# Fifty instead of thirty softmax tiles transposed by DMA, buffers named step by step, and a new order of steps

## The chip, the core and the metric

The kernel runs on one core of one Trainium2 chip. TensorE (PE) does the matrix products, VectorE (DVE), ScalarE (ACT) and GpSimd (POOL) the elementwise work, and SyncE (SP) issues nearly all DMAs. Every engine runs its own instructions in the order in which they are written, and waits on semaphores for the others. The metric is the time of one execution in device microseconds; lower is better.

## The reference, cut to what matters

Clustered attention (a query sees only the keys whose nearest centroid is the same as its own), then two feed-forward blocks on its output. Both weights and activations are float32, and the result has to keep nearly that precision.

```python
q_assign = np.argmax(np.einsum('bhsd,hcd->bhsc', q_n, c_n), axis=-1)   # B, H, S, D, C = 2, 8, 768, 64, 16
k_assign = np.argmax(np.einsum('bhsd,hcd->bhsc', k_n, c_n), axis=-1)
mask = q_assign[:, :, :, None] == k_assign[:, :, None, :]
scores = scale * np.matmul(q, k.transpose(0, 1, 3, 2))
scores = np.where(mask, scores, -1000000000.0)
scores = scores - np.max(scores, axis=-1, keepdims=True)
attn = np.exp(scores)
attn = attn / (np.sum(attn, axis=-1, keepdims=True) + 1e-09)
x = np.matmul(attn, v)             # then to [1536 tokens, 512]
h = x @ w_in                       # 512 x 2048
x = np.where(h > 0, h, np.exp(np.minimum(h, 0)) - 1) @ w_out
out = ((x @ w_a) * (x @ w_b)) @ w_out2   # 512 x 1536 twice, 1536 x 512
```

## The kernel before

**One list of steps.** The whole program is one list of words, `ORDER`, such as `tr:4.3.1`. A loop at the end of the kernel takes word after word and calls the function of that name with these numbers, which emits one step, on one engine or on SP's DMA queue. Nothing else orders the work: each engine runs its own steps in the order of the list, and a step waits only for the data and the buffers that it needs. A last number often says which engine takes the step: 0 is DVE, 1 ACT, 2 POOL.

**Attention.** There are 16 heads (batch times head), handled as 8 pairs, and each head has 6 tiles of 128 queries against all 768 keys, 96 tiles in all. For a tile `t` of head `g`:

- `sc` (PE, L673): the scores, four matmuls into one of two buffers in PSUM; the second two of them bring the cluster mask in.
- `rm` (DVE, L681): the negated row maximum.
- `ex` (ACT, L694): the exponential, float32, into `pf`, which has three buffers for all heads.
- Then the tile is split into two float16 parts, a high one and the remainder, and both are brought to keys-by-queries in `pt`, where the product with V reads them. This goes **one of two ways**.
  By PE: `tr` (PE, L727) transposes half of the tile, three 128x128 blocks, into PSUM; `th` (L731) copies that to float16 as the high part, and `tl` (DVE, L736) takes the remainder. A tile has two halves, so two `tr`, two `th`, two `tl`.
  By DMA: `hi` (L702, ACT or POOL) rounds the whole tile to float16 in `phl`, `lo` (POOL, L709) writes the remainder beside it, and `td` (SP, L741) is one DMA that transposes both parts into `pt`. Here `pf` stays taken until `lo` has read it.
- `av` (PE, L786): the product with V, for three tiles of both heads of a pair at a time (a "half", `f` 0 or 1), in three steps; `rb` (PE, L767) and `ev` (DVE) bring the division by the row sums in.

Besides these, each head needs its operands: `ka1`, `ka2` (the key and its rounding remainder, L523 and L530), `qa` (L545), `qb` (L484), `kbd` (a DMA), `vs`, `v1`, `v2` (V scaled and in two float16 parts, L491, L496, L501); `sm`, `st`, `m1` to `m5`, `oh`, `ohs`, `ohd` find the clusters.

**Weights.** Each weight comes in 68 pieces as int64 words (`wl`, a DMA). `wa` (ACT), `w0` to `w4` (DVE), `wh` (ACT), `ws` and `wq` (POOL, L905 and L911) turn a piece into a high and a low part. The first pieces are made during attention.

**The two MLPs.** `h`, `x2`, `ab` and `o` are the matrix products in three passes (high by high, low by high, high by low; L925 to L927).

Buffers come from `take`. A tag with several buffers hands them out in turn. The head of the program also has 60 steps `wm`, eight small matmuls each, that fill PE while it waits for the first data.

Of the kernel before, what the change touches and what calls it, by code (L numbers as in the profile page):

```python
# [65 lines left out]
lk:1.1 lk:0.0 wm:0 wm:2 lq:1.1 cz:0 lq:0.0 ib:0 wm:4 wm:6 cs:0 wm:7 wm:10 vl:2 wm:11 wl:0 mo:0 wm:15  # L66
kb:1 md:0 vl:3 wm:14 wm:19 ka1:0.1 vl:1 sb:0 wm:22 vl:0 ka1:1.1 kb:0 wm:25 wm:27 ka2:0.2 qa:1.1
ka2:1.0 wm:28 wm:29 wm:26 lk:2.0 c0:0 wm:33 qa:0.1 lk:3.0 wm:37 c1:0 ce:0 wm:38 qb:0 wm:5 wm:20 qb:1
wm:46 wm:48 c2:0 lq:2.0 vr:9 wm:24 wm:53 vr:10 wm:55 lq:3.0 vr:8 wm:17 vr:11 c3:0 wm:42 wa:0 c4:0
wm:49 wm:57 wm:23 wm:30 w0:0 sm:0.0 w1:0 vr:14 w2:0 vr:13 w3:0 sm:0.1 vr:12 w4:0 vr:15 sv:0.0.0 wh:0  # L70
wm:31 sv:0.1.0 wm:56 ws:0 vr:5 st:0 vr:6 vr:4 wq:0 wm:40 m1:0 vr:7 wm:13 m2:0 wm:45 vr:0 wm:16 m3:0
wm:1 vr:3 wl:1 m4:0 ka1:3.2 wm:39 vr:1 ka1:2.2 vr:2 vtp:0 m5:0 wm:18 wm:58 ka2:2.2 vtd:0 ot:0 oe:0
ot:2 wm:8 oe:2 wm:3 wm:47 wm:41 vbp:0 wm:52 sc:0.0 vbd:0 ot:3 rm:0.0 sc:0.1 qa:3.1 qa:2.1 wm:51
ka2:3.2 vs:1 wm:21 qb:2 ot:1 rm:0.1 oe:1 ex:0.0 oe:3 tr:0.0.1 sc:0.2 ex:0.1 rm:0.2 wa:1 qb:3 w0:1
wm:54 wm:50 lq:4.0 tr:0.1.0 th:0.0.1.1 sc:1.0 ex:0.2 th:0.1.0.1 hi:0.2.2 tl:0.0.1 wm:59 tr:0.0.0
sc:1.1 tl:0.1.0 rm:1.0 rm:1.1 tr:0.1.1 th:0.0.0.1 sm:1.0 th:0.1.1.1 vs:2 tl:0.1.1 ex:1.0 sc:1.2 vs:0
ex:1.1 tl:0.0.0 tr:1.0.1 sv:1.0.1 rm:1.2 th:1.0.1.1 vs:3 lo:0.2 w1:1 v1:0.1 sc:0.3 v2:0.2 kbd:3
rm:0.3 ex:1.2 wm:44 tl:1.0.1 w2:1 lq:5.0 tr:1.0.0 wm:12 th:1.0.0.1 v1:1.1 tr:1.1.0 th:1.1.0.1 sc:0.4
wm:9 tl:1.0.0 wm:36 rm:0.4 ra:0.0 ex:0.3 w3:1 w4:1 rc:0.0 tr:1.1.1 lk:4.0 th:1.1.1.1 sm:1.1 sc:0.5
hi:1.2.1 tl:1.1.1 ex:0.4 sv:1.1.1 wm:34 st:1 tl:1.1.0 rm:0.5 qa:4.1 wm:32 kbd:2 lo:1.2 ka1:4.2  # L80
v1:2.1 wh:1 ex:0.5 td:0.2 tr:0.3.0 sc:1.4 wm:35 rx:0.0 tr:0.3.1 sc:1.3 lk:5.0 th:0.3.0.1 m1:1
hi:0.5.1 m2:1 th:0.3.1.1 v2:1.2 v2:2.2 m3:1 m4:1 ka2:4.2 m5:1 tl:0.3.0 wm:43 oh:1 rm:1.3 ohs:1
tr:0.4.0 ex:1.3 tl:0.3.1 rm:1.4 ws:1 qb:4 th:0.4.0.1 td:1.2 av:0.0.0 rb:0.0 ohd:1 tr:0.4.1 sc:1.5
re:0.0.1 th:0.4.1.1 wl:2 tl:0.4.0 rm:1.5 tl:0.4.1 ex:1.4 qa:5.1 wq:1 tr:1.3.0 th:1.3.0.1 tr:1.3.1
av:0.0.1 th:1.3.1.0 tr:1.4.1 lq:7.0 ex:1.5 th:1.4.1.1 lo:0.5 ra:0.1 tl:1.3.1 sc:2.0 tl:1.3.0 rm:2.0
hi:1.5.1 tr:1.4.0 sc:2.1 ex:2.0 av:0.0.2 ka1:5.2 vs:4 lo:1.5 td:0.5 tl:1.4.1 rm:2.1 sc:2.2 tr:2.0.0
th:1.4.0.1 rc:0.1 tr:2.0.1 tl:1.4.0 ex:2.1 th:2.0.0.1 th:2.0.1.1 rx:0.1 lk:6.0 sc:3.0 rm:2.2 ex:2.2
# [1053 lines left out]
```

## Time and profile before

| | |
|---|---|
| Time, median of 3 runs | 818.26 us (817.41 to 818.92) |
| The profiled execution | 818.15 us |
| Its span, first to last instruction | 816.4 us |
| PE busy | 807.5 us, 99% of the span |
| DVE, ACT, POOL busy over the span | 592.6, 410.8, 340.7 us |
| Softmax tiles that go by DMA | 30 of 96 |

The span is the time between the first and the last instruction on the core; 1.75 us of the execution lie around it. The transposes of attention run from 33.9 us to 259.1 us, the products with V from 54.3 us, and the first product of the MLP begins at 252.6 us. Shares over the whole span mix two stages: after attention PE alone is full, while in attention the other engines are nearly full as well. So each stretch has to be read by itself.

### The profile page before, as it was taken

Reading aid. Unit: us, or ns where it says so; the run is one execution under the profiler, and the core shown is the slowest. Engines: PE = TensorE matmul, PEld = TensorE weight load, DVE = VectorE, ACT = ScalarE, POOL = GpSimd, SP = SyncE. Lnnn points to the kernel's source line nnn. Section 1 sums busy time; section 2 is a strip of 40 time slices with the busy share of each in tenths; the row PEclk is TensorE's granted clock in tenths of the full one; section 3 lists DMA queues with packets and bytes.
Section 4 is the critical chain, followed back from the end, with each engine's and each line's share of the span. In section 5 each row is a group of like instructions: output and inputs, shape, how many; then the busy total and the mean of one; then the engine's idle time right before and its main releaser. Section 6 shows DMA issues by size and latency. Waiting matters only on the chain.

```text
span 816.4 us, 12164 instructions
## 1 busy us (share of the span) xinstructions
PE 807.5 (99%) x4626; PEld 655.4 (80%) x4626; DVE 592.6 (73%) x876; ACT 410.8 (50%) x737; POOL 340.7 (42%) x295
## 2 busy tenths in 40 slices
...
GB/s 278 110 97 129 146 125 110 129 138 116 110 81 78 78 27 78 77 104 78 79 95 81 80 60 72 52 77 78 1 26 77 78 78 52 53 52 0 52 1 103
DMA packets 65626, 68.12 MB, mean 83 GB/s; under 512 B 49888, under 2 KB 49888, under 8 KB 65568
## 3 DMA queue, kind: packets, MB, share of 16 engines
q1 hardware_dynamic: 65328, 66.76, 30.6%
...
q10 hardware_dynamic: 240, 0.59, 0.3%
...
## 4 chain that ended last, share of the span: by engine, by line
PE 90%; POOL 5%; ACT 3%; issue 2%; DVE 0%; POOLq 0%; ACTq 0%
PE ab L927 8%; PE ab L925 8%; PE ab L926 8%; PE sc L673 6%; PE h L926 5%; PE h L925 5%; PE x L926 5%; PE x L925 5%; PE h L927 5%; PE x L927 5%; PE av L786 4%; PE o L927 4%; PE o L925 4%; PE o L926 4%; PE tt L727 4%; PE warm_ps L409 3%
## 5 line engine op out<-in xcount | busy, mean ns | idle before, releaser
L681 DVE TENSOR_REDUCE nm<-sc 128x1 f32<-128x768 f32 x96 | 90.8, 950 | 7.1 <-PE sc L673 6.0
L694 ACT ACTIVATE pf<-sc,nm 128x768 f32<-128x768 f32 x96 | 86.8, 905 | 15.7 <-POOL phl L709 6.9
L1027 ACT COPY t0ab<-ab 128x512 f32<-128x512 f32 x36 | 21.1, 587 | 108.5 <-PE ab L927 108.5
L736 DVE TENSOR_TENSOR pt<-tt,pt 128x384 f16<-128x384 f32 x132 | 70.0, 545 | 5.0 <-ACT pt L731 4.6
L1032 DVE TENSOR_TENSOR t1ab<-ab,t0ab 128x512 f32<-128x512 f32 x36 | 24.8, 688 | 63.2 <-ACT t0ab L1027 63.2
L727 PE MATMUL tt<-identf,pf 128*128 128x128 f32 x396 | 62.0, 277 | 1.4 <-ACT pf L694 1.4
L731 ACT CAST pt<-tt 128x384 f16<-128x384 f32 x122 | 55.9, 478 | 10.4 <-PE tt L727 9.8
L709 POOL TENSOR_TENSOR phl<-pf,phl 128x768 f16<-128x768 f32 x30 | 50.0, 1668 | 24.8 <-ACT phl L702 23.5
L673 PE MATMUL sc<-ka,qa 128*128 128x384 f32 x192 | 57.6, 381 | 2.5 <-ACT pf L694 2.4
L856 ACT ACTIVATE wg<-wraw 128x512 f32<-128x512 f32 x68 | 45.1, 667 | 25.5 <-DMA wraw<-in_w_out_dram 13.8
L727 PEld LDWEIGHTS tt<-identf,pf 128*128 128x128 f32 x396 | 46.0, 140 | 12.0 <-issue 4.3
L786 PE MATMUL av<-pt,v 128*64 128x384 f16 x576 | 52.7, 329 | 0.0
L873 DVE SCALAR_TENSOR_TENSOR wf<-wraw,wg 128x512 int32<-128x512 int32 x68 | 51.0, 751 | 1.8
L886 DVE SCALAR_TENSOR_TENSOR wg<-wraw,wg 128x512 f32<-128x512 uint32 x68 | 49.1, 723 | 1.7
L673 PE MATMUL sc<-kb,qb 80*128 80x384 f32 x192 | 49.6, 339 | 0.0
L1043 DVE TENSOR_TENSOR gl<-t1ab,gh 128x512 fp32r<-128x512 f32 x36 | 33.9, 941 | 18.7 <-ACT gh L1038 18.5
L861 DVE TENSOR_SCALAR wg<-wg 128x512 f32<-128x512 f32 x68 | 38.4, 566 | 8.8 <-ACT wg L856 8.6
L786 PEld LDWEIGHTS <-v 128*64 128x64 f16 x576 | 30.0, 109 | 18.4 <-issue 7.1
L866 DVE TENSOR_SCALAR wg<-wg 128x512 int32<-128x512 int32 x68 | 38.5, 567 | 1.8
L989 ACT CAST gh<-t1h 128x1024 fp32r<-128x1024 f32 x24 | 25.3, 1052 | 27.7 <-DVE t1h L981 27.7
L1083 DVE TENSOR_TENSOR acc<-o,acc 128x1024 f32<-128x1024 f32 (+1 forms) x12 | 14.2, 1180 | 32.3 <-PE o L927 32.3
L971 ACT ACTIVATE t0h<-h 128x1024 f32<-128x1024 f32 x24 | 24.6, 1024 | 23.3 <-PE h L927 23.2
...
## 6 DMA issues: line engine op xcount, KB each, us to landing
...
acc<-in_v_dram SPq DMA_DIRECT2D x4, 768.0 KB, 11.0
...
```

The costliest lines, as they stand in the source:

```text
L673: nc.tensor.matmul(s[:, j, :HALF], a[:, qs], b[:, j * HALF : (j + 1) * HALF], start=i == 0, stop=i == 1,)
L681: nc.vector.reduce_max(out=nm, in_=st[g][f"sc{t}"][:, :, :HALF], axis=AX.XY, negate=True)
L694: nc.scalar.activation(pf.rearrange("p (a b) -> p a b", a=2), st[g].pop(f"sc{t}")[:, :, :HALF], AF.Exp, bias=st[g].pop(f"nm{t}"), accum_ou ...
L709: nc.gpsimd.tensor_sub(phl[:, S:], st[g].pop(f"pf{t}"), phl[:, :S])
L727: nc.tensor.transpose(tt[:, k * P : (k + 1) * P], pf[:, o : o + P], identf)
L731: (nc.vector.tensor_copy, nc.scalar.copy)[e](next(parts_of(g, t, u)), st[g][f"tt{t}{u}"])
L736: nc.vector.tensor_sub(lo, st[g].pop(f"tt{t}{u}"), hi)
L786: nc.tensor.matmul(pairs[j]["av"][x * 64 : (x + 1) * 64].rearrange("p (a q) -> p a q", a=3), st[2 * j + x][("v1", "v2")[vi]][:, kt_, :], s ...
L873: nc.vector.scalar_tensor_tensor(out=f, in0=raws[n][:, :, 1], scalar=-0x40000000, in1=g, op0=ALU.bitwise_and, op1=ALU.bitwise_or,)
L925: nc.tensor.matmul(ps, lhi, rhi, start=first, stop=False)
L926: nc.tensor.matmul(ps, lhi, rlo, start=False, stop=False)
L927: nc.tensor.matmul(ps, llo, rhi, start=False, stop=last)
```

## The change

Twenty more tiles go by DMA: 50 of 96. The number of `td`, `hi` and `lo` rises from 30 to 50, and the number of `tr`, `th` and `tl` falls from 132 to 92, since each such tile has two halves. With them:

- `phl` has four buffers instead of three (`NPHL`).
- `qb` and `lo` get a last number for their engine. In the new list every `qb` stays on DVE and every `lo` on POOL.
- Some steps change engines: `hi` on ACT 12 to 34, on POOL 18 to 16. `th` on DVE 10 to 19. `ka1` on ACT 6 to 12, on POOL 10 to 4. `ka2` on DVE 1 to 6, on POOL 15 to 10. `v1` one from POOL to ACT, `sv` two and `re` three from DVE to ACT.
- A word may name buffers, as `sc:6.0/sc=0`. `take` then uses that buffer, and where a word names none, the next in turn.
- The list is in a new order. It has the same 60 `wm`, and the same number of every other step.

```diff
-NPHL = 3
+NPHL = 4
...
-qb:8 tr:4.4.0 th:4.4.1.1 sc:5.5 rm:5.4 tl:4.4.1 th:4.4.0.1 ka1:9.1 av:2.0.1 rm:5.5 tl:4.4.0 av:2.0.2
-rb:2.0 th:4.3.1.0 lo:4.5 lk:10.0 tr:5.3.0 ex:5.4 qa:9.1 ka2:9.2 ex:5.5 sc:6.0 kbd:7 tl:4.3.1
...
+ex:5.5/pf=2 ka2:9.0 rb:2.0/tt=1 hi:4.5.1/phl=2 qb:9.0 sc:6.0/sc=0 lq:11.0/rawq=1 w3:3 hi:5.5.1/phl=0
...
+    named, taken = {}, {}
+
     def take(pool, tag, shape, dt, name, bufs=1):
-        return pool.tile(shape, dt, tag=tag, bufs=bufs, name=name)
+        if bufs > 1:
+            n = taken[tag] = int(named.pop(tag, (taken.get(tag, -1) + 1) % bufs))
+            tag = f"{tag}_{n}"
+        return pool.tile(shape, dt, tag=tag, bufs=1, name=name)
...
-    def minus_scaled(out, a, scale, b):
-        nc.vector.scalar_tensor_tensor(
+    def minus_scaled(e, out, a, scale, b):
+        (nc.vector, None, nc.gpsimd)[e].scalar_tensor_tensor(
...
-    def lo(g, t):
+    def lo(g, t, e):
         phl = st[g][f"phl{t}"]
-        nc.gpsimd.tensor_sub(phl[:, S:], st[g].pop(f"pf{t}"), phl[:, :S])
+        (nc.vector, None, nc.gpsimd)[e].tensor_sub(phl[:, S:], st[g].pop(f"pf{t}"), phl[:, :S])
...
-    for word in ORDER.split():
+    for line in ORDER.split():
+        word, *buffers = line.split("/")
+        named.update(n.split("=") for n in buffers)
         name, args = word.split(":")
```

What the new list does is seen best on single engines. The place shown is the same on all three: the second half of the third pair (heads 4 and 5), at whose end head 6 begins. In a name such as `pf4_5_1991` the 4 is the tile, the 5 the head, and the last number only tells buffers apart. Line numbers after the change are 39 higher in this part of the program.

PE before, from the `rb` of that pair's first half on:

```order
L767 MATMUL rbp_2_0_1979<-identf_89,rx_2_0_1901 128x128 x3
L727 MATMUL tt30_5_1987<-identf_89,pf3_5_1925 128x128 x3
L673 MATMUL sc0_6_1998<-ka_6_1431,qa_6_1409 128x384 x2
L673 MATMUL sc0_6_1998<-kb_6_1855,qb_6_1573 128x384 x2
L727 MATMUL tt40_5_2007<-identf_89,pf4_5_1991 128x128 x3
L673 MATMUL sc1_6_2013<-ka_6_1431,qa_6_1409 128x384 x2
L673 MATMUL sc1_6_2013<-kb_6_1855,qb_6_1573 128x384 x2
L727 MATMUL tt31_5_2029<-identf_89,pf3_5_1925 128x128 x3
```

and after:

```order
L806 MATMUL rbp_2_0_1939<-identf_89,rx_2_0_1887 128x128 x3
L712 MATMUL sc0_6_1947<-ka_6_1443,qa_6_1445 128x384 x2
L712 MATMUL sc0_6_1947<-kb_6_1723,qb_6_1507 128x384 x2
L712 MATMUL sc1_6_1967<-ka_6_1443,qa_6_1445 128x384 x2
L712 MATMUL sc1_6_1967<-kb_6_1723,qb_6_1507 128x384 x2
L612 MATMUL sm_4_0_1981<-qa_8_1794,cq1_106 64x384
```

Transposes of tiles 3 and 4 of head 5 stood around the first scores of head 6. Tile 4 has left PE, tile 3 stands further ahead, and the first two scores of head 6 follow each other at once.

POOL before, between the two `rx` of the same pair (L709 is `lo`, L702 `hi`, L530 `ka2`):

```order
L757 COPY rx_2_0_1901<-rs_2_0_1770 128x384
L530 TENSOR_TENSOR ka_8_1868<-rawk_8_1797,ka_8_1868 64x768
L491 TENSOR_TENSOR acc_66<-acc_66,vsc_112 128x384
L709 TENSOR_TENSOR phl5_4_1932<-pf5_4_1870,phl5_4_1932 128x768
L530 TENSOR_TENSOR ka_9_1950<-rawk_9_1841,ka_9_1950 64x768
L702 CAST phl5_5_2021<-pf5_5_1996 128x768
L496 CAST v1_7_2026<-acc_66 128x384
L491 TENSOR_TENSOR acc_66<-acc_66,vsc_112 128x384
L709 TENSOR_TENSOR phl5_5_2021<-pf5_5_1996,phl5_5_2021 128x768
L491 TENSOR_TENSOR acc_66<-acc_66,vsc_112 128x384
L757 COPY rx_2_1_2102<-rs_2_1_2046 128x384
```

and after, between the same two `rx` (L748 is `lo`; here L530 is `vs`):

```order
L796 COPY rx_2_0_1887<-rs_2_0_1755 128x384
L748 TENSOR_TENSOR phl5_4_1943<-pf5_4_1810,phl5_4_1943 128x768
L530 TENSOR_TENSOR acc_66<-acc_66,vsc_112 128x384
L748 TENSOR_TENSOR phl5_5_1956<-pf5_5_1936,phl5_5_1956 128x768
L748 TENSOR_TENSOR phl4_5_1991<-pf4_5_1920,phl4_5_1991 128x768
L796 COPY rx_2_1_2038<-rs_2_1_1974 128x384
```

Three `lo` instead of two, two of them back to back, and the two `ka2` are gone from between: that of head 8 stands earlier on POOL, that of head 9 is on DVE.

DVE before, around the `qb` of head 9 (L736 is `tl`, L681 `rm`):

```order
L681 TENSOR_REDUCE nm4_5_1946<-sc4_5_1887 128x1
L736 TENSOR_TENSOR pt1_4_1908<-tt41_4_1897,pt1_4_1908 128x384
L681 TENSOR_REDUCE nm5_5_1964<-sc5_5_1941 128x1
L736 TENSOR_TENSOR pt1_4_1908<-tt40_4_1936,pt1_4_1908 128x384
L731 CAST pt1_4_1908<-tt31_4_1893 128x384
L736 TENSOR_TENSOR pt1_4_1908<-tt31_4_1893,pt1_4_1908 128x384
L484 SCALAR_TENSOR_TENSOR qb_9_2018<-rawq_9_1616,qa_9_1993 64x768
L736 TENSOR_TENSOR pt1_5_2005<-tt30_5_1987,pt1_5_2005 128x384
L681 TENSOR_REDUCE nm0_6_2024<-sc0_6_1998 128x1
L736 TENSOR_TENSOR pt1_5_2005<-tt40_5_2007,pt1_5_2005 128x384
L681 TENSOR_REDUCE nm1_6_2044<-sc1_6_2013 128x1
```

and after (L775 is `tl`, L720 `rm`, L569 `ka2`):

```order
L720 TENSOR_REDUCE nm4_5_1859<-sc4_5_1850 128x1
L775 TENSOR_TENSOR pt1_4_1833<-tt31_4_1789,pt1_4_1833 128x384
L720 TENSOR_REDUCE nm5_5_1885<-sc5_5_1862 128x1
L523 SCALAR_TENSOR_TENSOR qb_8_1918<-rawq_8_1566,qa_8_1794 64x768
L569 TENSOR_TENSOR ka_9_1880<-rawk_9_1725,ka_9_1880 64x768
L523 SCALAR_TENSOR_TENSOR qb_9_1945<-rawq_9_1814,qa_9_1934 64x768
L920 TENSOR_SCALAR wg3_1489<-wf3_1490 128x512
L775 TENSOR_TENSOR pt1_5_1871<-tt30_5_1867,pt1_5_1871 128x384
L720 TENSOR_REDUCE nm0_6_1963<-sc0_6_1947 128x1
L720 TENSOR_REDUCE nm1_6_1972<-sc1_6_1967 128x1
```

The `tl` of tiles 4 of heads 4 and 5 are gone, and `ka2` of head 9, which subtracts two tiles that both lie in SBUF, has come to stand between the two `qb`.

## Rows read from the trace of the kernel before

**Rows 1.** The page, section 1: PE over the span, busy us (share) xinstructions.
```profile
PE 807.5 (99%) x4626; PEld 655.4 (80%) x4626; DVE 592.6 (73%) x876; ACT 410.8 (50%) x737; POOL 340.7 (42%) x295
```

**Rows 2.** Busy time of each engine by stretch of the span (us).
```profile
core 0: us, PE busy (x) PEld busy (x) DVE busy (x) ACT busy (x) POOL busy (x), PEclk, DMA share, GB/s
54.00:268.00 214.00, 209.92 (x1590) 159.52 (x1591) 197.38 (x331) 180.05 (x381) 136.45 (x123) 1.00 0.53 115
80.00:240.00 160.00, 157.53 (x1208) 119.64 (x1203) 149.21 (x248) 137.56 (x297) 109.83 (x101) 1.00 0.58 121
```

**Rows 3.** Waits from 54 to 268 us: us in total, times, longest.
```profile
ACT pf L694 <- POOL phl L709: 6.9, 6, 1.9
...
PEld sc L673 <- ACT pf L694: 5.3, 10, 1.1
```

**Rows 4.** The chain that ended last, 54 to 268 us: shares of the stretch.
```profile
by line: PE sc L673 21.3%; PE av L786 15.7%; PE tt L727 14.3%; PE sm L573 6.8%; issue 6.4%; POOL phl L709 5.3%; ACT pf L694 4.9%; PE rbp L767 3.3%; POOL ka L530 2.9%; POOL phl L702 2.5%; ACT pt L731 1.9%; PE h L925 1.7%; PE h L927 1.7%; PE 
```

**Rows 5.** The same chain from 160 to 180 us: start us, us, what.
```profile
160.61 0.33 PE tt L727 x3
...
169.07 1.66 POOL phl L709
...
170.75 1.00 ACT pf L694 x2
```

**Rows 6.** Timeline of PE beside the last transposes: start us, us, what.
```profile
258.18 1.14 PE L727 MATMUL tt<-identf,pf 128*128 128x128 f32 x9
259.08 0.48 PE L925 MATMUL h<-x0h,w0h 128*128 128x512 f32 x1
```

**Rows 7.** Transposes as a group, PE, 54 to 268 us.
```profile
L727 PE MATMUL tt<-identf,pf 128*128 128x128 f32 x366 | 56.9, 278 | 1.4 <-ACT pf L694 1.4
```

**Rows 8.** Groups of POOL by shape, 33 to 270 us.
```profile
L709 POOL TENSOR_TENSOR phl<-pf,phl 128x768 f16<-128x768 f32 x30 | 50.0, 1668 | 24.8 <-ACT phl L702 23.5 <-POOL ka L530 0.2
L530 POOL TENSOR_TENSOR ka<-rawk,ka 64x768 fp32r<-64x768 f32 x12 | 21.9, 1823 | 7.2 <-PE tt L727 3.5 <-ACT ka L523 2.9
L702 POOL CAST phl<-pf 128x768 f16<-128x768 f32 x18 | 17.4, 966 | 26.9 <-ACT pf L694 22.7 <-issue 2.2 <-POOL ka L530 1.9
...
L523 POOL CAST ka<-rawk 64x768 fp32r<-64x768 f32 x8 | 6.5, 817 | 0.6 <-PE sc L673 0.6
```

**Rows 9.** Groups of ACT by shape, 33 to 270 us.
```profile
L731 ACT CAST pt<-tt 128x384 f16<-128x384 f32 x122 | 55.9, 478 | 10.4 <-PE tt L727 9.8
...
L702 ACT CAST phl<-pf 128x768 f16<-128x768 f32 x12 | 10.0, 837 | 0.0
```

**Rows 10.** Groups of DVE by shape, 33 to 270 us.
```profile
L736 DVE TENSOR_TENSOR pt<-tt,pt 128x384 f16<-128x384 f32 x132 | 70.0, 545 | 5.0 <-ACT pt L731 4.6
L484 DVE SCALAR_TENSOR_TENSOR qb<-rawq,qa 64x768 fp32r<-64x768 f32 x14 | 13.3, 955 | 1.5 <-ACT qa L545 1.5
...
L731 DVE CAST pt<-tt 128x384 f16<-128x384 f32 x10 | 5.5, 548 | 2.3 <-PE tt L727 2.3
```

**Rows 11.** Timeline at the start: one DVE instruction beside one of POOL.
```profile
5.96 1.81 POOL L530 TENSOR_TENSOR ka<-rawk,ka 64x768 fp32r<-64x768 f32 x1 [1.38 <-ACT ka L523]
...
6.64 1.95 DVE L530 TENSOR_TENSOR ka<-rawk,ka 64x768 fp32r<-64x768 f32 x1 [4.11 <-ACT ka L523]
```

**Rows 12.** One DVE line of the MLP: ns minimum/median/maximum, first and last start.
```profile
L996 DVE TENSOR_TENSOR gl<-t1h,gh x24: 1210/1218/2325, 266.8 to 503.8; 128x1024 fp32r<-128x1024 f32 x24
```

**Rows 13.** The DMA transposes: issue ns minimum/median/maximum; us from issue to landing.
```profile
L741 SPq DMA_TRANSPOSE pt<-phl x30: 1275/1440/2931, 42.1 to 241.7; - x30
...
DMA to landing us min/median/max: 3.6/3.8/5.5
```

**Rows 14.** Timeline of POOL before the second matrix product of the first MLP.
```profile
262.97 1.29 POOL L911 TENSOR_TENSOR w1l<-wf,wg 128x512 fp32r<-128x512 f32 x1
...
273.33 1.29 POOL L911 TENSOR_TENSOR w1l<-wf,wg 128x512 fp32r<-128x512 f32 x1 [1.33 <-DVE wg L886]
```

**Rows 15.** Timeline of PE where that product begins.
```profile
279.46 0.39 PE L925 MATMUL x<-gh,w1h 128*128 128x512 f32 x1
```

More of the change, by code (lines that the diff above doesn't have):

```diff
@@ L65 @@
 ORDER = """
[L66 to L87, printed above, removed]
@@ new lines @@
+ka2:2.2 m2:0 vr:3 vr:1 wm:45 wm:16 wm:1 wm:39 wm:18 vr:2 m3:0 m4:0 ka1:3.1 m5:0/oht=0 vtp:0/tt=1
+wm:58 wq:0 vtd:0 wm:8 wl:1 wm:3 wm:47 qa:3.1 ot:0/tt=2 qa:2.1 ot:2/tt=0 vbp:0/tt=1 oe:0 ka2:3.2 oe:2
+vbd:0 wm:41 wm:52 sc:0.0/sc=0 qb:2.0 rm:0.0/nm=0 ot:3/tt=2 vs:2 vs:4 wa:1 ot:1/tt=0 sc:0.1/sc=1
+ex:0.0/pf=0/sum=0 vs:0 wm:51 oe:1 vs:3 rm:0.1/nm=1 wm:21 tr:0.0.0/tt=1 oe:3 w0:1 vs:1 sc:0.2/sc=0
+rm:0.2/nm=2 kbd:2 wm:54 wm:50 w1:1 ex:0.1/pf=1 wm:59 qb:3.0 sc:1.1/sc=1 tr:0.1.0/tt=0
+th:0.0.0.1/pt=0 v1:2.1/v1=0 ex:0.2/pf=2 sc:1.0/sc=0 lk:4.0/rawk=1 tl:0.0.0 hi:0.2.1/phl=0 th:0.1.0.1
@@ new lines @@
+oh:2/tt=0 ev:0.1 tr:2.3.0/tt=1 ka1:6.1 qa:6.1 hi:2.4.1/phl=2 wl:3 rm:3.3/nm=1 lo:2.5.2 re:1.0.1/rb=0
+th:2.3.0.0/pt=2 ohs:2/ohs=1 wq:2 lq:7.0/rawq=0 sc:3.4/sc=0 av:1.0.0 ex:3.3/pf=0 ka2:6.2
+tr:2.3.1/tt=2 wa:3 rm:3.4/nm=2 sc:3.5/sc=1 th:2.3.1.1 lk:7.0/rawk=0 ohd:2 tl:2.3.0 qb:6.0
+tr:3.3.0/tt=0 ex:3.4/pf=1 av:1.0.1 lo:2.4.2 ka1:7.1 av:1.0.2 tl:2.3.1 th:3.3.0.0/pt=3 rm:3.5/nm=3
+tr:3.3.1/tt=1 w0:3 qa:7.1 sc:4.0/sc=0 ex:3.5/pf=2 th:3.3.1.1 td:2.4 ka2:7.0 qb:7.0 lq:8.0/rawq=1
+sc:4.1/sc=1 hi:3.5.1/phl=0 rm:4.0/nm=0 tl:3.3.1 hi:3.4.1/phl=3 ex:4.0/pf=0/sum=0 rm:4.1/nm=1
```

372 lines of the change are left out of this document (208 added, 164 removed).

## The prediction

> **What bounds the kernel now.** I read the page first: PE is busy for 807.5 us of a span of 816.4 us [rows 1], with the clock granted in full (1.00 in both stretches of [rows 2]). So the time is PE's, and I look for where it is not. The table by stretch shows it: in attention's main part, 54 to 268 us, PE is busy for 209.92 of 214 us, so it stands idle for 4.1 us there, and this is nearly all of its idle time after the start. The reader should also see the columns beside it: DVE 197.4 us (92%), ACT 180.1 (84%), POOL 136.5 (64%), DMA 53%. PE is the bound, but two engines are close behind, and in the steady part, 80 to 240 us, POOL is at 109.8 of 160 (69%) [rows 2].
>
> The list of waits tells what PE's few idle microseconds hang on. The scores wait 5.3 us for ACT's `ex` (a free score buffer), and `ex` in turn waits 6.9 us for POOL's `lo` (a free `pf`) [rows 3]. The chain of work says the same: the `tt` transposes hold 14.3% of the stretch, but `lo` 5.3%, `ka2` 2.9% and `hi` 2.5% on POOL are on it too [rows 4]. One such passage stands at 169.07 us: `lo` for 1.66 us, then `ex`, which waited for it [rows 5]. So two chains run close together: PE's own work, and `ex`, `lo`, the next `ex`. The change shortens the first and lengthens the second.
>
> **What PE loses.** Twenty tiles, two `tr` each, three transposes each: 40 groups, 120 transposes. On the chain a group of three takes 0.33 us [rows 5]. Nine in a row take from 258.18 to 259.08, 0.90 us, so 0.30 us a group [rows 6]. I take 0.315: **40 x 0.315 = 12.6 us** off PE. From below the bound is 40 x 0.30 = 12.0; from above the group's busy time, 56.9 us for 122 groups [rows 7], 0.466 us each, 18.7 in all; that counts the tail of each group, which lies under the next matmul, so I stay near the low end. The `wm` are as many as before, also behind the first score, so the start keeps its length.
>
> **What the other engines gain and lose**, against the 214 us that would become 214 - 12.6 = 201.4:
>
> DVE: 40 `tl` less at 0.545, -21.8; nine `th` more at 0.548, +4.9; five small copies less at about the same 0.548, -2.7 [rows 10]. Five `ka2` more have no steady row on DVE. From below each costs what `qb` costs, of the same shape and with two inputs in SBUF, 0.955 [rows 10]; from above 1.95, the one `ka2` that DVE has now [rows 11]: +4.8 to +9.7. Sum 182.6 to 187.5, 91 to 93% of 201.4: as close as before.
>
> ACT: 49 `th` less at 0.478, -23.4; 22 `hi` more at 0.837, +18.4 [rows 9]; six `ka1` more, taken at the price of `hi` for the same 768 columns, +5.0; six small copies at 0.478, +2.9. Sum 183.0, now 91% instead of 84%. What covered the ACT waits is thinner.
>
> POOL: 20 `lo` more at 1.668, +33.4; two `hi` less at 0.966, six `ka1` less at 0.817, five `ka2` less at 1.823, together -16.0 [rows 8]; one `v1` less at about half a `ka1`, -0.4. Sum 153.5, 76% instead of 64%. POOL becomes busier in the steady part above all, since nothing is added in the last pair.
>
> SP and DMA: 20 transposes more, 1.44 us of SP each and 3.8 us from issue to landing [rows 13]. If each held all DMA engines for its whole 3.8 us, this would be 76 us on top of 0.53 x 214 = 113 us, 189 of 201: an upper bound, and not over. I cost it at nothing, because a `td` is asked for by `av` several tiles later; without that cover it costs what a rival below does.
>
> The fourth `phl` and the named buffers I cost at nothing: no row of waits names `phl`'s buffers, so a gain has no place to come from, and the wait for `pf` is untouched, since it still has three.
>
> **How much of the 12.6 us is given back.** Two ways, neither of which a row settles. From below: nothing, PE idles 4.1 us as now. From above: the transposes' share on the chain is 14.3% of 214, 30.6 us, of 122 x 0.315 = 38.4 us; so a fifth of PE's saving lies where the other chain is as late, 2.5 us; and the added `lo` lengthen that chain: 11.3 us (5.3%) for 28 `lo` of the stretch, 20 more are 8.1 us, less 5 of 12 `ka2` there, 2.6 of the 6.2 us (2.9%), 5.5 in all [rows 4]. Together 8.0. Between 0 and 8.0 no row is nearer to one end, so I take the middle, 4.0.
>
> Sum: the profiled execution took 818.15 us, 0.1 under the median of 818.26. **818.15 - 12.6 + 4.0 = 809.6 us.**
>
> The MLP behind it is PE without a gap, and moves forward as a block. The place to fear is the second product: the last piece of its weight is ready at 273.33 + 1.29 = 274.6 us [rows 14], the product begins at 279.46 [rows 15], 4.8 us later. Such pieces come 10.4 us apart [rows 14]. If the new list were one piece behind there, it would cost 5.6 us; since both the attention steps and the pieces' steps move forward by the same, I take nothing.
>
> **The rivals.**
>
> *POOL's chain takes over, and the kernel gets slower.* Mechanism: `pf` is held until `lo` has read it, `lo` stands in POOL's queue behind `rx`, `vs`, `v2`, `ka2`, and the next `ex` and the next scores wait. Now 28 tiles of the stretch cost `ex` 6.9 us [rows 3], 0.25 each. With 48 tiles it decides at (12.6 + 6.9) / 48 = 0.41 us each, if all of it reaches PE. At 0.6, about a third of a `lo` of waiting in the queue, the loss is 48 x 0.6 - 6.9 = 21.9, and the time 818.15 - 12.6 + 21.9 = 827.5. For it: POOL at 76% in a queue kept in order. Against it: POOL waits itself now, 24.8 us before `lo` and 26.9 before `hi` [rows 8], so the load fits in. Chance 0.13.
>
> *DVE stands behind POOL.* The DVE `ka2` started at 6.64 us, while POOL's ran from 5.96 to 7.77, and took 1.95 us: so it ended 0.82 after POOL's, little less than the 0.955 of a `qb` by itself [rows 10, 11]. In the MLP one subtraction of the same kind takes 1.22 us in the median, but up to 2.33 [rows 12]. So a DVE instruction with two inputs in SBUF waits for a running POOL instruction. After the change five more `ka2` and the 14 `qb` of the main part meet a POOL that is busier; if 19 wait 1.0 us each, DVE comes to 182.6 + 19 = 201.6, as much as the stage has. With PE's present share of busy time, 98%, DVE would need 205.7 us, 8.3 under the present 214: 809.9; with `ka2`, which the scores need, late as well by 1.0 us six times, 815.9. Chance 0.10.
>
> By the Trainium skill, page "SBUF — State Buffer", section "Who interferes with whom", a VectorE instruction with two SBUF inputs contends with a GpSimd instruction that reads SBUF, and whichever issues first holds the shared port for its whole length. The trace agrees in its 1.95 us; `tl`, with one input in PSUM, is free by the same rule, and its 0.545 us agree. Going by the rule alone, with each of the 19 waiting half a `lo`, 0.83 us, the sum would be 818.15 - 12.6 + 15.8 = 821.4 if all of it reached PE.
>
> *The landing takes the gain.* There are 16 halves, and each `av` needs the last landing of its six tiles. Now the median landing is 3.8 us, the worst 5.5 [rows 13]. If three `td` of a half stand in line and the last is 1.7 us late in half of the 16, 13.6 us go back: 819.2, no change. Against it: no row shows PE waiting for a landing in the stretch. Chance 0.06.
>
> *Nothing is given back.* DVE has less to do, and PE's idle time falls with the transposes' own waits (1.4 us of it stand before `tt` [rows 7]): 818.15 - 12.6 - 1.4 = 804.2. Chance 0.11.
>
> **How the numbers follow.** My forecast, a gain of 5 to 13 us, has 0.60. Faster by over 0.2% (1.6 us, about what a measurement of this kernel can tell from no change): 0.60 + 0.11 + 0.10 = 0.81. No change: the landing, 0.06. Slower: 0.13. The range goes from 803.5, where nothing is given back, to 817.5: it takes in the port's 815.9 and leaves out the slower rival and the larger part of the landing's.
>
> **What would show it.** In the profile after: 276 transposes on PE instead of 396; attention's end, the first `h`, some 9 us before 252.6; PE idle 6 to 10 us between 54 and there; `ex` waiting for `lo` longer than 6.9 us in all; `ka2` on DVE at 1.0 to 2.0 us; landings with a median near 4; the MLP without a gap, the second product not waiting for its weight. I am wrong if PE's idle time in attention passes 17 us, or if a gap stands before that product.

## The result, and the profile after

The changed kernel takes 805.53 us (median of 4 runs, 804.4 to 806.13), the kernel before 817.84 us beside it (817.29 to 818.92). The ratio is 0.9846, with a 95% interval from 0.9829 to 0.9863: 12.3 us faster. The profiled execution took 804.4 us, 13.75 less than that of before.

The page of the changed kernel, section 1: PE over the span, to set against [rows 1].

```profile
span 802.6 us, 11967 instructions
...
PE 794.1 (99%) x4506; PEld 642.9 (80%) x4506; DVE 589.5 (73%) x845; ACT 414.7 (52%) x722; POOL 359.8 (45%) x301
```

PE is still the bound. It is busy 13.4 us less, and idle for 8.5 us of the span instead of 8.9. So the span is 13.8 us shorter, and nearly all of that is work that PE no longer has.

Busy time by stretch, as in [rows 2]; attention's main part now ends at 255 instead of 268 us. The third row is the stretch in which the second matrix product begins.

```profile
core 0: us, PE busy (x) PEld busy (x) DVE busy (x) ACT busy (x) POOL busy (x), PEclk, DMA share, GB/s
54.00:255.00 201.00, 198.66 (x1486) 148.86 (x1485) 190.90 (x305) 181.38 (x365) 149.80 (x125) 1.00 0.79 159
80.00:230.00 150.00, 147.97 (x1113) 109.70 (x1113) 142.43 (x225) 138.06 (x281) 124.06 (x105) 1.00 0.87 173
255.00:300.00 45.00, 45.00 (x200) 37.24 (x199) 33.57 (x42) 22.10 (x26) 14.52 (x10) 1.00 0.19 59
```

In the main part PE stands idle for 2.3 us (201 - 198.66), where it was 4.1. All four engines are fuller: DVE at 95%, ACT at 90%, POOL at 75%, in the steady part at 83%, and the DMA engines at 0.79, where it was 0.53. In the third row PE has no gap.

Waits from 54 to 255 us: us in total, times, longest. These answer to [rows 3].

```profile
PEld sc L712 <- ACT pf L733: 2.7, 7, 0.9
...
PE av L825 <- DMA pt<-phl: 1.3, 2, 1.0
...
POOL phl L748 <- DMA pt<-phl: 1.2, 1, 1.2
...
ACT pf L733 <- POOL phl L748: 0.3, 1, 0.3
```

The wait that the slower rival was built on, `ex` for `lo`, has not grown from 6.9 us: it has all but gone, 0.3. New is `av` waiting for a landing, 1.3 us in two places. The 1.2 us that the profile puts between a landing and `lo` (at 157.57 us) are no wait for a free `phl`: ACT's `hi` had been writing that same `phl` since 156.66, and `lo` began when it was done. So with four buffers nothing waited for one.

```profile
156.66 0.83 ACT L741 CAST phl<-pf 128x768 f16<-128x768 f32 x1
...
157.57 2.33 POOL L748 TENSOR_TENSOR phl<-pf,phl 128x768 f16<-128x768 f32 x1 [1.22 <-DMA pt<-phl]
```

The chain that ended last, 54 to 255 us, shares of the stretch by line, as in [rows 4], and its longest piece off PE.

```profile
by line: PE sc L712 28.3%; PE av L825 21.0%; PE tt L766 13.9%; PE sm L612 10.9%; PE rbp L806 4.8%; DMA pt<-phl 2.6%; PE h L964 2.0%; PE h L965 1.9%; PE h L966 1.8%; PE tp L626 1.5%; issue 1.5%; DVE nm L720 1.4%; DMA kb<-ohs 1.1%; ACT pf L73
...
155.71 5.18 DMA pt<-phl
```

`lo` and `hi` on POOL, 7.8% before, are not among the lines that are shown; DVE's `rm` has 1.4%, a landing 2.6%. The chain is in the main PE's own work.

The steps of `phl`, and then DVE's `ka2`: ns minimum/median/maximum, first and last start, as in [rows 8, 11, 13].

```profile
L748 POOL TENSOR_TENSOR phl<-pf,phl x50: 1642/1651/2351, 38.6 to 226.5; 128x768 f16<-128x768 f32 x50
L780 SPq DMA_TRANSPOSE pt<-phl x50: 1289/1463/2875, 40.3 to 228.1; - x50
...
DMA to landing us min/median/max: 3.7/4.1/6.5
```
```profile
L569 DVE TENSOR_TENSOR ka<-rawk,ka x6: 951/952/1947, 6.6 to 190.7; 64x768 fp32r<-64x768 f32 x6
```

The landings are a little later than the 3.6/3.8/5.5 us of before, and `lo` is 1.65 in the median as it was. The six `ka2` of DVE have a median of 0.952 us, and only the first, which stood in the kernel before too, takes 1.95. But the longest `lo` went up, from 1.92 to 2.35 us, and the reason is the port rival the other way round: two of the five added `ka2` did run beside a `lo`, and since the `ka2` had begun first, it was the `lo` that took longer (the other is the `lo` at 157.57 above, whose `ka2` began at 157.44).

```profile
136.60 0.95 DVE L569 TENSOR_TENSOR ka<-rawk,ka 64x768 fp32r<-64x768 f32 x1
136.77 2.30 POOL L748 TENSOR_TENSOR phl<-pf,phl 128x768 f16<-128x768 f32 x1 [2.11 <-issue]
```

Four more `lo` began behind a `qb` and took 2.07 to 2.35 us. The six together are 3.6 us over the median, paid by POOL, and `ex` still waited for `lo` only 0.3 us.

PE where the first product of the MLP begins: start us, us, what.

```profile
238.28 0.48 PE L964 MATMUL h<-x0h,w0h 128*128 128x512 f32 x1
```

That is 14.4 us earlier than the 252.6 us of before; the last transpose starts at 250.5 instead of 259.1, 8.6 us earlier.

### The profile page after: what moved, and what is told of

Same layout as the page of the kernel before. It is cut to its first block, busy times and chain, and to the rows that moved or that the text cites. A ratio compares the mean times of both kernels' runs of the same rounds, so it can differ in the third digit from the quotient of the medians.

```text
span 802.6 us, 11967 instructions
## 1 busy us (share of the span) xinstructions
PE 794.1 (99%) x4506; PEld 642.9 (80%) x4506; DVE 589.5 (73%) x845; ACT 414.7 (52%) x722; POOL 359.8 (45%) x301
## 3 DMA queue, kind: packets, MB, share of 16 engines
HBM read 48.27 MB, written 3.15 MB: 64 GB/s over the span
## 4 chain that ended last, share of the span: by engine, by line
PE 95%; DVE 2%; DMA 1%; ACT 1%; issue 0%; POOL 0%; SPq 0%; ACTq 0%; POOLq 0%
PE ab L966 8%; PE ab L964 8%; PE ab L965 8%; PE sc L712 8%; PE h L964 5%; PE h L965 5%; PE x L965 5%; PE x L964 5%; PE h L966 5%; PE x L966 5%; PE av L825 5%; PE o L966 4%; PE o L964 4%; PE o L965 4%; PE tt L766 4%; PE sm L612 4%
## 5 line engine op out<-in xcount | busy, mean ns | idle before, releaser
L748 POOL TENSOR_TENSOR phl<-pf,phl 128x768 f16<-128x768 f32 x50 | 86.1, 1724 | 30.5 <-ACT phl L741 23.0
L720 DVE TENSOR_REDUCE nm<-sc 128x1 f32<-128x768 f32 x96 | 90.5, 950 | 6.3 <-PE sc L712 5.0
L895 ACT ACTIVATE wg<-wraw 128x512 f32<-128x512 f32 x68 | 45.2, 669 | 27.0 <-DMA wraw<-in_w_out_dram 11.5
L912 DVE SCALAR_TENSOR_TENSOR wf<-wraw,wg 128x512 int32<-128x512 int32 x68 | 52.7, 776 | 1.9
L925 DVE SCALAR_TENSOR_TENSOR wg<-wraw,wg 128x512 f32<-128x512 uint32 x68 | 51.3, 755 | 1.7
L775 DVE TENSOR_TENSOR pt<-tt,pt 128x384 f16<-128x384 f32 x92 | 49.1, 547 | 2.0 <-ACT pt L770 1.5
L766 PE MATMUL tt<-identf,pf 128*128 128x128 f32 x276 | 44.1, 278 | 1.0 <-ACT pf L733 0.7
L1020 DVE SCALAR_TENSOR_TENSOR t1h<-t0h,h 128x1024 f32<-128x1024 f32 x24 | 29.2, 1216 | 17.3 <-ACT t0h L1015 17.2
L766 PEld LDWEIGHTS tt<-identf,pf 128*128 128x128 f32 x276 | 31.9, 140 | 10.2 <-issue 2.9
L770 ACT CAST pt<-tt 128x384 f16<-128x384 f32 x73 | 33.7, 475 | 5.8 <-PE tt L766 5.4
```

What stands on the lines that cost most here:

```text
L720: nc.vector.reduce_max(out=nm, in_=st[g][f"sc{t}"][:, :, :HALF], axis=AX.XY, negate=True)
L748: (nc.vector, None, nc.gpsimd)[e].tensor_sub(phl[:, S:], st[g].pop(f"pf{t}"), phl[:, :S])
L766: nc.tensor.transpose(tt[:, k * P : (k + 1) * P], pf[:, o : o + P], identf)
L775: nc.vector.tensor_sub(lo, st[g].pop(f"tt{t}{u}"), hi)
L912: nc.vector.scalar_tensor_tensor(out=f, in0=raws[n][:, :, 1], scalar=-0x40000000, in1=g, op0=ALU.bitwise_and, op1=ALU.bitwise_or,)
L925: nc.vector.scalar_tensor_tensor(out=g, in0=raws.pop(n)[:, :, 0].bitcast(U32), scalar=2.0 ** -52, in1=g, op0=ALU.mult, op1=ALU.mult,)
```

## The experiments

Each kernel ran beside the kernel before; the ratio is to that. "Busy" and "idle" are PE's busy time and the span less that, from the page of the profiled run. The last column is the granted clock from 54 to 255 us. Where it is under 1.00, PE's busy time holds more than the instructions: PE then did the same work for a while at the lower of its two clocks (1.2 instead of 2.4 GHz). So a time over that of its base has two parts, PE's longer idle time and this.

| kernel | median us | ratio [95%] | busy | idle | clock |
|---|---|---|---|---|---|
| before | 817.84 | | 807.5 | 8.9 | 1.00 |
| changed | 805.53 | 0.9846 [0.9829, 0.9863] | 794.1 | 8.5 | 1.00 |
| e3: changed, 40 `tr` twice | 814.4 | 0.9954 [0.9939, 0.9969] | 805.5 | 6.8 | 1.00 |
| b1: before, 40 `tr` twice | 831.64 | 1.0166 [1.0149, 1.0183] | 820.7 | 9.5 | 0.99 |
| e2: old order, 50 tiles by DMA | 851.89 | 1.0413 [1.0397, 1.0429] | 813.5 | 36.5 | 0.92 |
| e1: new order, 30 tiles by DMA | 875.61 | 1.0704 [1.0646, 1.0762] | 831.5 | 40.4 | 0.94 |
| e5: changed, three `phl` | 815.51 | 0.9959 [0.9941, 0.9977] | 796.5 | 13.2 | 1.00 |
| e9: changed, 13 `hi` to POOL | 814.51 | 0.9957 [0.9942, 0.9971] | 800.8 | 12.7 | 0.97 |
| e8: changed, five `ka2` to POOL | 808.99 | 0.9895 [0.9881, 0.991] | 797.5 | 10.7 | 0.99 |
| e6: changed, 20 `lo` twice | 835.42 | 1.0227 [1.0203, 1.0251] | 805.7 | 27.1 | 0.96 |
| b2: before, 20 `lo` twice | 845.69 | 1.0342 [1.0318, 1.0365] | 823.9 | 22.5 | 0.92 |
| e7: changed, 20 `td` twice | 862.55 | 1.0547 [1.0531, 1.0563] | 815.8 | 44.2 | 0.91 |
| b3: before, 20 `td` twice | 861.27 | 1.0534 [1.0519, 1.055] | 822.0 | 38.9 | 0.92 |
| e11: changed, 55 tiles by DMA | 826.9 | 1.0107 [1.0066, 1.0148] | 803.2 | 17.8 | 0.95 |

### What PE's work is worth: e3 and b1

Forty groups of transposes are done twice, in the changed kernel and in that of before. PE gets back as many instructions as the change took from it, and no other engine has more to do.

```diff
-        for k in range(3):
-            o = u * HALF + k * P
+        for k in range(6 if (g, t, u) in TWICE else 3):
+            o = u * HALF + k % 3 * P
```

**Expected of e3:** 

> The changed kernel, with 40 of its tr done twice over (three transposes, and the same three again into the same place): 120 transposes more on PE, as many as the change took away, and nothing more on any other engine. Theory A (PE is the only bound after the change): 40 x 0.315 to 40 x 0.344, 12.6 to 13.8 us longer, 818 to 819 us. Rival (the other chains are as close, PE's added work hides in part): less than 7 us longer, under 812.5 us.

Measured: 814.4 us, 8.9 more than the changed kernel. The page and the stretch:

```profile
PE 805.5 (99%) x4626; PEld 655.8 (81%) x4626; DVE 590.8 (73%) x845; ACT 415.8 (51%) x722; POOL 359.5 (44%) x301
```
```profile
54.00:255.00 201.00, 200.39 (x1536) 154.33 (x1536) 183.81 (x291) 175.72 (x355) 146.96 (x123) 1.00 0.79 156
```

PE has the 4626 instructions of before. It is busy 11.4 us more (0.285 per group), and its idle time falls by 1.7 us, to 0.6 in the main part; together this is the 9.7 us by which the span grew. The 40 groups stand directly behind their first copy, which is the cheapest place for them. Summed over the trace from each transpose's start to the start of PE's next instruction, the transposes take 41.4 us in e3 and 28.8 in the changed kernel, 12.6 more (in the kernel before 42.6).

**Expected of b1:** 

> The kernel before, with 40 of its tr done twice: 120 transposes more on PE, nothing more elsewhere. In the changed kernel the same edit cost 8.9 us. Prediction's reading (PE is the bound before, with POOL's chain close behind): 9 to 12.6 us longer, 827 to 831. Rival (PE's work is as much hidden before as its 4.1 us of idle time allows, or a transposed tile's wait passes on to DVE and ACT): 13 us or more, over 831.

Measured: 831.64 us, 13.9 more than before, with 13.2 us more busy time. That is on the rival's side of the expectation (over 831), and e3's 8.9 lies between its two theories. In b1 a part is the clock: after an idle of 2.43 us, in which the scores waited for `ex`, it fell for a short stretch.

```profile
90.00:94.00 4.00, 4.00 (x32) 2.41 (x30) 3.56 (x5) 3.71 (x8) 1.05 (x1) 0.57 0.09 21
```

PE works without a gap there, so 0.57 of the clock in 4 us is 1.7 us lost. Without it the 40 groups add 11.5 us of busy time, as in e3 (11.4). So in either list they are some 11.4 us of PE's work; in time they cost 13.9 in the list before and 8.9 in the new one. And with as much work for PE as before, the new list takes 814.4 instead of the 818.3 us of the kernel before beside it: some 4 us of the 12.3 belong to the order and to the work's new places, at most, since e3's groups have the cheapest place.

### Order against number of tiles: e2 and e1

e2 keeps the old order and engines, and sends the same 20 tiles by DMA: `hi` (on ACT) takes the place of the tile's first `th`, `lo` of its first `tl`, `td` of its second. It has four `phl`.

```diff
-tr:5.4.0 th:5.4.0.1 tl:5.4.0 tr:5.4.1 th:5.4.1.1 tl:5.4.1
+hi:5.4.1 lo:5.4 td:5.4
```

**Expected:** 

> The kernel before in its old order and with its old engines, but the same twenty tiles go by DMA as after the change: hi on ACT where the first th stood, lo on POOL where the first tl stood, td where the second tl stood, and four phl. Theory A (only PE's work counts): 818 - 12.6 to 818 - 13.8, 804 to 806 us. Theory B (without the new order POOL's chain lengthens, as the prediction's upper bound for what is given back and its slower rival had it): 8.0 to 21.9 us given back, 812 to 827 us, and ex waits for lo longer than 6.9 us.

Measured: 851.89 us. The waits from 54 to 255 us:

```profile
PEld sc L665 <- ACT pf L686: 15.4, 19, 3.6
...
ACT pf L686 <- POOL phl L701: 14.8, 12, 3.4
PE av L778 <- DMA pt<-phl: 14.7, 8, 3.2
PEld L778 <- DMA pt<-phl: 13.6, 7, 3.4
```

Both waits that the rivals spoke of are here: `ex` for `lo`, 14.8 us, and `av` and its weight load for the landing, up to 3.4 us at a time, at 8 places. PE does the work of the changed kernel and is idle 28.0 us longer. It is also busy 19.4 us longer with the same instructions, at a granted clock of 0.92 in the main part. The time lies far over both theories (804 to 806, and 812 to 827). So the slower rival's mechanism is real; with the old order it decides, together with the landing and the lower clock.

e1 goes the other way: the new order, with the 20 tiles back on PE. Each half's `tr`, `th`, `tl` stand behind each other, in the places of `hi` and `lo`.

```diff
-hi:5.4.1/phl=1
+tr:5.4.0/tt=2 th:5.4.0.1 tl:5.4.0
...
-lo:5.4.2
-td:5.4
+tr:5.4.1/tt=0 th:5.4.1.1 tl:5.4.1
```

**Expected:** 

> The changed kernel, but the twenty added tiles go back to PE: where their hi and lo stood there are again two halves of tr, th and tl, and their td is gone. All else keeps the new order, its engines and its buffers. Theory A (the gain is PE's transposes and nothing else; between the two traces PE's time in transposes and idle fell by 13.8 us): 805.5 + 13.8 = 819 us, as before the change. Theory B (the new order and the new places of ka2 and hi removed POOL's chain, on which ex waited 6.9 us before and 0.3 after, and the transposes alone give little): at most 812 us.

Measured: 875.61 us. Waits from 54 to 255 us:

```profile
ACT pt L778 <- PE tt L774: 28.4, 28, 3.0
DVE pt L783 <- ACT pt L778: 24.1, 25, 2.5
...
PEld tt L774 <- DVE pt L783: 14.9, 17, 1.4
```

This fits neither theory (819, or at most 812). Each `th` waits for its `tr`, each `tl` for its `th`, and the next `tr` for that `tl`. This tells nothing of the number of tiles, since these steps stand closer together than in either list. It shows what the list does when it is right: it keeps a lead between a step and the one that needs it. A tile's way decides which steps it has, so its number and the order are not fully told apart by e1 and e2; e3 is the cleaner measure.

### What keeps `lo` from being late: e5, e9 and e8

e5 has three `phl` instead of four. So that three suffice, five `hi` stand later (behind the `td` that frees a buffer), and four `td` or `lo` are moved with them.

```diff
-NPHL = 4
+NPHL = 3
```

**Expected:** 

> The changed kernel with three phl instead of four; for this, five hi stand later in the list, each behind the td that frees a buffer. Prediction's step (the fourth phl costs and gives nothing): within 1 us of 805.5. Rival (50 tiles need the fourth, hi waits for landings of 4.1 us, and pf with it): five places, up to 4.1 us each, 3 to 20 us longer, and hi waits for landings in the trace.

Measured: 815.51 us, 10.0 more than the changed kernel (the profiled run took 811.57). Waits from 54 to 255 us:

```profile
PEld sc L712 <- ACT pf L733: 6.3, 10, 2.3
...
ACT pf L733 <- POOL phl L748: 4.2, 6, 1.7
...
ACT phl L741 <- DMA pt<-phl: 2.4, 2, 1.4
```

`hi` now waits for a landing, `lo` comes later behind it, `ex` waits 4.2 us for `lo`, and the scores for `ex`. The mean granted clock of the whole execution was 1.00 in three of the ten, which took 810.9 to 811.6 us, and 0.990 to 0.994 in the seven others, which took 814.8 to 816.7. So with the full clock three buffers cost 5.4 us, and the rest of the 10.0 comes with a lower clock. That is nearly half of the gain, or most of it where the clock falls, with the later places of the five `hi` counted in.

e9 puts the 13 `hi` that ACT does for added tiles on POOL, at the same place in the list. e8 puts the five `ka2` back on POOL.

```diff
-hi:5.4.1/phl=1
+hi:5.4.2/phl=1
```
```diff
-ka2:9.0
+ka2:9.2
```

**Expected of e9:** 

> The changed kernel, with hi of those 13 added tiles that have it on ACT put on POOL, in the same place of the list: 13 x 0.84 = 11 us more on POOL, as much less on ACT. Theory A (neither engine bounds): within 2 us of 805.5. Theory B (POOL is the closer chain, and taking hi off it is a part of why nothing was given back): 3 to 11 us longer, and ex waits for lo again, over the 0.3 us that it waits now.

Measured: 814.51 us, 9.0 more. The wait from 54 to 255 us, and three stretches in the middle:

```profile
ACT pf L733 <- POOL phl L748: 6.9, 7, 2.8
```
```profile
130.00:143.00 13.00, 11.40 (x92) 8.27 (x91) 12.05 (x14) 10.43 (x19) 12.78 (x10) 1.00 0.69 154
143.00:150.00 7.00, 7.00 (x24) 4.98 (x23) 5.61 (x10) 3.82 (x9) 5.57 (x6) 0.52 1.15 178
160.00:164.00 4.00, 4.00 (x24) 2.35 (x24) 3.85 (x7) 2.62 (x7) 3.92 (x5) 0.57 1.42 171
```

The 13 casts bring `ex` back to 6.9 us of waiting for `lo`. More is lost than PE's idle time shows: of the 10.9 us by which the span grew, 4.2 are idle and 6.7 are busy time with the same instructions. The second and third row show where most of the 6.7 went. From 143 to 150 us PE works without a gap, but at 0.52 of the clock, so 3.4 us are lost; from 160 to 164 us it is 0.57, and 1.7. What stood ahead of the first, on the timeline:

```profile
139.01 4.56 POOL L748 TENSOR_TENSOR phl<-pf,phl 128x768 f16<-128x768 f32 x2
...
139.77 2.29 DVE L569 TENSOR_TENSOR ka<-rawk,ka 64x768 fp32r<-64x768 f32 x1
...
142.10 0.56 DVE L775 TENSOR_TENSOR pt<-tt,pt 128x384 f16<-128x384 f32 x1
...
142.71 0.39 PE L612 MATMUL sm<-qa,cq 128*64 128x384 f32 x1 [1.60 <-DVE pt L775]
```

One `ka2` of DVE (0.95 in the changed kernel) takes 2.29 us while POOL does two `lo`. These take 4.56 us, where two take 3.3 by the median. The `tl` behind the `ka2` starts when it is done, PE waits 1.60 us for that `tl`, and then the clock falls. This is the rival "DVE stands behind POOL". It is met a second time at 199.72 us, where a `ka2` that began behind a `lo` took 2.13. Ahead of the second fall it is POOL's chain instead: `ex` waits 2.82 us for `lo`, and PE 2.14 us for `ex`.

```profile
158.99 0.62 PE L712 MATMUL sc<-ka,qa 128*128 128x384 f32 x2 [2.14 <-ACT pf L733]
```

**Expected of e8:** 

> The changed kernel, with the five ka2 that went to DVE back on POOL, in the same place of the list: 5 x 1.82 = 9.1 us more on POOL, 5 x 0.95 = 4.8 less on DVE. Theory B (POOL is the closer chain, and taking work off it is a part of why nothing was given back): 5 to 10 us longer, 810 to 816, as 11 us of hi cost 9. Rival (the port: DVE and POOL block each other less without these ka2): shorter than 805, or the same.

Measured: 808.99 us, 3.5 more, less than the 5 to 10 that were expected. `ex` waits again, and the scores longer than the 2.7 us of the changed kernel:

```profile
PEld sc L712 <- ACT pf L733: 5.0, 9, 1.7
...
ACT pf L733 <- POOL phl L748: 1.2, 3, 0.5
```

Five instructions of 1.82 us are 9.1 us of POOL; a good third of that shows in the time, and about half of this third is the clock: from 119 to 123 us PE works without a gap at 0.57 of it, 1.7 us lost. The `ka2` on DVE are worth their place.

### How much room is left: e6, b2, e7, b3 and e11

In the changed kernel the `lo` of the 20 added tiles is done twice (e6), or their `td` (e7). In the kernel before the same is done to 20 of its 30 (b2, b3). One reading, theory D of the expectations, is that the list before had room for more of these steps; the other is that in each list every step stands just as early as it is needed.

```diff
+        pf = st[g].pop(f"pf{t}")
+        for _ in range(2 if (g, t) in TWICE else 1):
+            (nc.vector, None, nc.gpsimd)[e].tensor_sub(phl[:, S:], pf, phl[:, :S])
```
```diff
+        phl = st[g].pop(f"phl{t}")
+        for _ in range(2 if (g, t) in TWICE else 1):
+            nc.sync.dma_start_transpose(out=pt_of(g, f)[:, a], in_=phl)
```

**Expected of e6:** 

> The changed kernel, with lo of the twenty added tiles done twice (the same remainder written again): 20 x 1.67 = 33 us more on POOL, whose busy time from 54 to 255 us would go from 150 to 183 of 201, and nothing more elsewhere. Theory A (PE is the bound, POOL has room): within 2 us of 805.5. Theory B (POOL's chain from lo to ex is close behind, as doubling tr showed that some chain is within 4 us): over 4 us longer, up to 20 x 1.67 = 33 if all of it shows.

**Expected of b2:** 

> The kernel before, with 20 of its 30 lo done twice: 33 us more on POOL, nothing more elsewhere. In the changed kernel as much cost 30 us. Theory D (POOL had room before, which the change used up): under 15 us longer, below 833. Theory E (the old order was bound by POOL's chain as well, as its place in the chain of work says, and the new order is no nearer to POOL than the old): 25 to 33 us longer, 843 to 851.

Measured: e6 835.42 us, 29.9 more than the changed kernel; b2 845.69, 28.0 more than before. The wait of `ex`, in e6 and then in b2:

```profile
ACT pf L734 <- POOL phl L751: 15.7, 14, 2.3
```
```profile
ACT pf L695 <- POOL phl L712: 26.7, 12, 5.4
```

Twenty `lo` are 33 us of POOL, and they cost nearly as much time in either list, although POOL is busy for only 75% of the main part in the one and 64% in the other [rows 2]. About half of the cost is waiting: PE's idle time grows by 18.6 us in e6 and by 13.6 in b2. The rest, 11.6 and 16.4 us, is busy time with the same instructions, at a granted clock of 0.96 and 0.92. Free time on an engine is no room where its next step is due at once.

**Expected of e7:** 

> The changed kernel, with the DMA transpose of the twenty added tiles issued twice (same data, same place): nothing more on any engine, 20 x 1.46 = 29 us more on SP's queue, and by the growth of the DMA share between the two traces (0.53 x 214 us with 28 transposes, 0.79 x 201 with 48) 2.3 us of all DMA engines each, 46 us on 159 of 201. Theory A (the landing is hidden): within 2 us of 805.5. Theory C (the DMA queue is next to full, the product with V waits for landings): 10 to 46 us longer, with waits of av for landings well over the 2.6 us of the changed kernel.

**Expected of b3:** 

> The kernel before, with 20 of its 30 td issued twice: 29 us more on SP's queue and 46 us more of the DMA engines, on 113 of 214. In the changed kernel as much cost 57 us. Theory D (the DMA engines had room before): under 10 us longer, below 828. Theory E (each later landing shows in the product with V at once, full engines or not, since the list puts av where the landing is due): 20 to 57 us longer, 838 to 875.

Measured: e7 862.55 us, 57.0 more; b3 861.27, 43.6 more. The waits of `av` for the landing, in e7 and in b3:

```profile
PE av L828 <- DMA pt<-phl: 22.9, 8, 5.7
```
```profile
PE av L789 <- DMA pt<-phl: 19.8, 4, 7.7
```

The edit does more than the expectations say. The second transpose writes the same place as the first, and SP issues it only when the first has landed. The waits of SP, over the whole span, in e7 and in b3:

```profile
SPq L783 <- DMA pt<-phl: 52.1, 20, 3.9
```
```profile
SPq L744 <- DMA pt<-phl: 50.9, 20, 3.7
```

So SP stands for some 2.6 us at each of the 20, on top of the 1.46 of the issue, with the later DMAs of its queue behind it, and the tile arrives a whole issue and landing later. The 57.0 and 43.6 us are the price of that (the first is over the 46 of Theory C), not of the load of 20 more transposes. In b3 `av` waits up to 7.7 us while the DMA engines are busy for only 0.69 of 54 to 255 us (0.89 in e7): a late landing shows at once, with nearly a third of the DMA time free. What a second transpose that need not wait would cost is not shown. Theory D (below 833 in b2, below 828 in b3) fits neither run.

e11 sends five more tiles by DMA (2.1, 4.1, 6.1, 8.1, 10.1).

```diff
-tr:4.1.0/tt=1 th:4.1.0.1 tl:4.1.0 tr:4.1.1/tt=0 th:4.1.1.1 tl:4.1.1
+hi:4.1.1/phl=3 lo:4.1.2 td:4.1
```

**Expected:** 

> The changed kernel with five more tiles by DMA, 55 of 96 (tile 1 of heads 2, 4, 6, 8 and 10; hi on ACT at the first tr, lo on POOL at the second, td at the second tl): 10 groups less on PE. Theory A (PE bounds, 12.6 us of its work cost 8.9): 2.2 to 3.2 us shorter, 802.3 to 803.3. Theory C (POOL at 79% and the DMA engines at 85% in the main part leave no room): no gain or longer, 805 to 812.

Measured: 826.9 us (822.77 to 830.54), 21.4 more than the changed kernel. Waits from 54 to 255 us:

```profile
PEld sc L710 <- ACT pf L731: 11.1, 19, 1.7
...
PE av L823 <- DMA pt<-phl: 4.8, 3, 1.9
```

That is over both theories (802.3 to 803.3, and 805 to 812). In the profiled execution PE is idle 9.3 us longer, and busy 9.1 us longer with 30 instructions less, at a granted clock of 0.95. Put into the list as it is, five more tiles cost far more than the 3.15 us that they take off PE. Whether a list made for 55 would be faster stays open. No version that was run beats the changed kernel.

## Why the prediction was right, and where it was not

**PE's price held.** The sum took 12.6 us off PE. PE's busy time fell by 13.4, its transposes are 276, and in e3 as many groups took 12.6 us more from start to start. This term carries the result. What such work is worth in time is less sharp: 40 groups cost 8.9 us in e3, where they stand in pairs and fill some idle time, and 13.9 in b1, of which 1.7 is a lower clock. One reading of the rows was loose, without bearing on the sum: of PE's 8.9 idle us, 4.1 lie in attention's main part, but 3.7 at the very end, behind 810 us.

**"Given back" was mis-sized.** Between 0 and 8.0 the prediction took 4.0, so 809.6. In the profiled executions 13.75 us were gained, in the medians 12.3: nothing, or 0.3, was given back. The argument was that the added `lo` lengthen the chain through `ex`, and that `ex` would wait for `lo` longer than 6.9 us. It waits for 0.3. The mechanism is there, since e2, e6, e8 and e9 each bring the wait back (1.2 to 15.7 us) and lose 3.5 us and more; but the prediction carried today's wait over to a list that puts these steps elsewhere. It counted the moves to DVE and ACT as load, not as what takes a step out of the queue ahead of `lo`: 13 `hi` on ACT are worth 9.0 us, five `ka2` on DVE 3.5, lower clock included.

**"The fourth `phl` at nothing" was wrong.** The reason given was that no wait in the trace of before names `phl`'s buffers. That was true with 30 tiles and says nothing of 50: with three buffers the time is 815.5 (e5), and 5.4 us over the changed kernel's where the clock stays full.

**The order was taken as neutral, and is not.** With the old order the same 20 tiles give 851.9 us (e2). With as much work on PE as before, the new list is some 4 us faster (e3). How much of the 4 us is the order and how much the other engines' new load is not settled, nor what the named buffers give: a list without names was not run. This point and "given back" are not two separate errors, though. If the 40 groups are worth the 8.9 us of e3, then 3.7 of the 12.6 were given back, close to the 4.0, and the order and the new places brought the same 4 us in again. That the time came out 4 us under the forecast is shown; whether "given back" was too large or the order's gain was left out depends on where the line is drawn, and no run settles it.

**The landing cost next to nothing here**, 1.3 us in two places, where the sum had nothing. But the cover that the prediction named, "several tiles later", is thin: `av` waits for a landing up to 3.2 us in e2 and 1.9 in e11, and in e7 and b3, where each doubled landing comes a whole transpose later, up to 7.7. That rival had its chance for the right reason.

**The rival by the port.** The five `ka2` on DVE took 0.952 us each, the lower of the two bounds, and DVE did not become the bound. That is not because they never met a `lo`: two did, and had begun first, so the `lo` took 2.30 and 2.33 us instead of 1.65. In e9 two `ka2` began second and took 2.29 and 2.13. So the prediction looked at one side only: who pays is a matter of who begins first, and in the changed kernel POOL pays, 3.6 us in six `lo`, with no wait of `ex` to show for it. The Trainium skill, page "SBUF — State Buffer", section "Who interferes with whom", says that the order of issue decides which of the two blocks. The four cases here agree, and so does the 1.95 at the start [rows 11].

**The loads.** POOL came to 149.8 us (153.5 expected), ACT to 181.4 (183.0), DVE to 190.9, above the 182.6 to 187.5 that were expected. A part of this is that weight steps with two inputs in SBUF took longer, for instance 0.896 instead of 0.685 us in the mean of six for one of them; the rest is not accounted for. The MLP moved forward as a block, without a gap before the second product, as expected.

**The signs named beforehand.** Right: 276 transposes, the landings near 4, the MLP, and the `ka2` at 0.95, just under the 1.0 to 2.0. The first `h` came earlier, but by 14.4 us instead of some 9. Wrong: PE's idle time in attention fell to 2.3 us instead of growing to 6 to 10, and `ex` waits less for `lo`, not more.
